# An adaLN transformer block on one core: Silu from PSUM, softmax without its maximum, one V transfer a tile, and a new order from a table of priorities

## The chip, the cores and the metric

The kernel runs on one core of a Trainium2 chip. The metric is the device time of one execution in microseconds. The kernel before took 284.76 us (median of 3 runs, 284.24 to 285.57).

Engines are named as in the profile: PE is the matrix engine, PEld its weight load, DVE the vector engine, ACT the scalar engine, POOL GpSimd, and SP the engine whose queue issues all DMA transfers here.

## The reference

Sequence 2048, model width 512, 32 heads of 16, FFN width 1792, all in bf16. A conditioning vector gives shift, scale and gate for each half of the block. Each token attends to 8 positions: itself and every second one before it.

```python
x = A_x
mod = (_silu(c) @ w_mod).reshape(c.shape[0], 6, 1, -1)
sa, ca, ga, sb, cb, gb = (mod[:, 0].copy(), ..., mod[:, 5].copy())
h = _layernorm(x, axis=-1) * (1 + ca) + sa
x = x + ga * _A_ref(h, A_wqkv, A_wo)
h = _layernorm(x, axis=-1) * (1 + cb) + sb
x = x + gb * _B_ref(h, B_w1, B_w3, B_w2)

# in _A_ref: W, dil = 8, 2
idx = pos[:, None] - off[None, :]            # off = arange(W) * dil
logits = jnp.einsum('bhsd,bhswd->bhsw', q, kg) * scale
attn = _softmax(jnp.where(mask, logits, -1e9), axis=-1)
o = jnp.einsum('bhsw,bhswd->bhsd', attn, vg)  # then @ wo
# in _B_ref
h = _silu(gate) * up                          # gate = x @ w1, up = x @ w3
out = jnp.einsum('bsf,fd->bsd', h, w2)
```

## The kernel before, in words

The work is cut into 16 tiles of 128 tokens and 4 chunks of 4 tiles. x stays in SBUF (`x_sb`).

**LN1 and projections, for each chunk.** DVE takes statistics (L520, L521), POOL the reciprocal root (L527, L529), DVE the norm (L536); PE transposes (L550) and ACT evicts with scale and shift (L558) into `h`. PE then computes q and k transposed (L585) and V by token (L604); ACT evicts them (L592, L593, L614). V goes to a scratch tensor in DRAM.

**Attention, for each tile.** DVE multiplies q with 8 shifted views of k in one instruction of 4096 columns (`sb_pq`, L633). PE sums over each head's 16 rows with an indicator matrix, 32 small matmuls (L642), into logits of 8 x 32 columns. DVE takes their maximum over a token (L652), ACT the exponential with that as bias (L655), DVE sum (L660), reciprocal (L663) and product (L665). The weights go to DRAM and come back laid out by (token, neighbour) on partitions (`sb_al`). V is read back in the same layout (`sb_vsh`): partition 8 s + w holds, for each of 8 groups g, the row of token 16 g + s minus 2 w. That takes 8 DMAs of 128 KB a tile. DVE multiplies weights into V (L680, again 4096 columns), PE sums over the neighbours with 32 small matmuls (L689), ACT evicts (L695), PE applies `wo` (L701, with the gate already multiplied in), and DVE adds to x (L705).

**FFN, for each chunk.** After LN2 of the 4 tiles come 14 units. In each, PE computes gate and up (L717, 4 matmuls of 512 columns each, into two PSUM banks); ACT evicts tanh(gate / 2) (L723) and up (L725); DVE forms (tanh + 1) * gate from PSUM (L727) and the product with up (L730). This is twice Silu(gate) * up; the half is in the gate `gb` (L514). W2 then takes 14 matmuls a tile (L741), and DVE adds x (L747) and SP stores.

**What sets the order.** Every operation is given an engine, a cost and a priority (`pr`). `Program.schedule` plays the program through with these costs: when an engine is free, it takes the operation of lowest `pr` whose inputs are ready and whose buffers (`Pool`) are free. The order that comes out is fixed for each engine; `synchronize` adds semaphore waits, and each engine runs its list strictly in order, SP too (all DMAs are issued at L123). Priorities before are formulas: attention of tile T at 1000 T, the FFN of a chunk 5500 behind its start, and so on. Buffers: 3 for `sb_vsh`, 3 for q, 6 for the normed x, 8 PSUM banks.

Of the kernel before, what the change touches and what calls it, by code (L numbers as in the profile page):

```python
# [11 lines left out]
P = 128  # L12
# [17 lines left out]
DMA_RATE = 260.0  # L30
# [31 lines left out]
class Op:  # L62
    __slots__ = ("eng", "fn", "cost", "pr", "deps", "vals", "n", "start", "end", "seen", "pos", "dma", "bytes",
                 "waits", "inc", "clock", "prev", "group")

    def __init__(self, eng, fn, cost, pr):
        self.eng, self.fn, self.cost, self.pr = eng, fn, cost, pr
        self.deps = {}
        self.vals = []
        self.prev = []  # L70
        self.end = None
        self.dma = False
        self.bytes = 0
        self.inc = None
        self.group = [self]


class Program:
# [7 lines left out]
    def op(self, eng, fn, cost, pr, r=(), w=(), part=(), after=(), dma=0):  # L86
        o = Op(eng, fn, cost, pr)
# [28 lines left out]
    def dma(self, out, in_, pr, nbytes, r=(), w=(), part=(), after=(), eng="sp", cost=450, group=None):  # L116
        nc = self.nc

        def fn(e):
            a = out() if callable(out) else out  # L120
            b = in_() if callable(in_) else in_
            with nc.allow_non_contiguous_dma(reason="layout"):
                return e.dma_start(a, b)  # L123

        o = self.op(eng, fn, cost, pr, r=r, w=w, part=part, after=after, dma=nbytes)
        if group is not None:
            group.append(o)
            o.group = group
        return o

    def schedule(self):
        ops = self.ops
        users = {o: [] for o in ops}
        missing = {}
        for o in ops:
            missing[o] = len(o.deps)
# [5 lines left out]
        ready_at = {o: 0 for o in ops}  # L142
        for o in ops:
            if not missing[o]:
                heapq.heappush(waiting[o.eng], (o.pr, o.n, o))
        busy = {e: 0 for e in ENGINES}
        self.order = {e: [] for e in ENGINES}
        self.placed = []
        dma_free = 0
        events = [0]  # L150
        done = []
        now = 0
        count = 0
        while count < len(ops):
            if not events:
                stuck = [(e, [(o.pr, o.n, [v.name for v in o.vals]) for _, _, o in sorted(waiting[e])[:3]]) for e in ENGINES]
                raise RuntimeError(f"stuck at {now}: {stuck}")
# [3 lines left out]
            while done and done[0][0] <= now:  # L161
                _, _, o = heapq.heappop(done)
                for v in o.vals:
# [3 lines left out]
                for u in users[o]:  # L167
                    missing[u] -= 1
                    ready_at[u] = max(ready_at[u], now)
                    if not missing[u]:  # L170
                        heapq.heappush(waiting[u.eng], (u.pr, u.n, u))
            for e in ENGINES:
                if busy[e] > now or not waiting[e]:
                    continue
                skipped, got = [], None
                while waiting[e]:
                    item = heapq.heappop(waiting[e])
                    o = item[2]
# [4 lines left out]
                    if all(len(p.free) >= k for p, k in need.items()):  # L183
                        got = o
                        break
                    skipped.append(item)
                for item in skipped:
                    heapq.heappush(waiting[e], item)
                if got is None:
                    continue  # L190
                o = got
                for v in o.vals:
# [3 lines left out]
                o.start = now  # L196
                busy[e] = now + o.cost
                if o.dma:
                    begin = max(now + o.cost, dma_free)
                    dma_free = begin + o.bytes / DMA_RATE  # L200
                    o.end = dma_free + LAT["sp"]
                else:
                    o.end = now + o.cost + LAT[e]
# [6 lines left out]
                count += 1  # L210
# [73 lines left out]
def bass_adaLN_cond__sliding_local_dilated__glu_gated_swiglu__prompt_kernel(  # L284
# [3 lines left out]
    with ctx:  # L288
        p = Program(nc, ctx)
        _build(p, *[_full_ap(t) for t in (A_x, A_wqkv, A_wo, B_w1, B_w3, B_w2, c, w_mod, out)])  # L290
        p.schedule()
# [4 lines left out]
MM = 216  # L296


def _build(p, A_x, A_wqkv, A_wo, B_w1, B_w3, B_w2, c, w_mod, out):
# [23 lines left out]
    atb = [sb([P, W, H], bf, f"attn{i}") for i in range(2)]  # L323
    alb = [sb([P, 8, H], bf, f"al{i}") for i in range(3)]
    exb = [sb([P, W, H], f32, f"ex{i}") for i in range(2)]
# [12 lines left out]
    smx = sb([P, 2], f32, "smx")  # L338
    ssum = sb([P, 2, H], f32, "ssum")
    rsum = sb([P, 2, H], f32, "rsum")  # L340
# [8 lines left out]
    NHH, NTMP = 20, 5  # L349
    region = sb([P, 1024 * NHH + 2048 * NTMP], dt.uint8, "region")  # L350
# [6 lines left out]
    thb = [at([P, 512], bf, f"th{i}", 1024 * NHH + 2048 * i) for i in range(NTMP)]  # L357
    ubb = [at([P, 512], bf, f"ub{i}", 1024 * NHH + 2048 * i + 1024) for i in range(NTMP)]
# [3 lines left out]
    wm_g = [at([P, KT, 512], bf, f"wm_g{i}", 12288 * i + 8192) for i in range(2)]  # L362

# [15 lines left out]
    smpool = Pool("sm", [(atb[i], exb[i], i) for i in range(2)])  # L379
    alpool = Pool("al", alb)  # L380
    otpool = Pool("ot", otb)
    hhpool = Pool("hh", hhb)
    tmppool = Pool("tmp", [(thb[i], ubb[i]) for i in range(NTMP)])

    TT = 1000.0

    def t_attn(T):
        return TT * T

    def t_ffn(cch, fi):  # L390
        return TT * (4 * cch + 5.5) + fi * (4 * TT / 20)

    def t_w2(T):
        return TT * (4 * (T // 4) + 5.5) + (14 + 1.5 * (T % 4)) * (4 * TT / 20)


    vc = Val("const")
    vident = Val("ident")
    p.op("pool", lambda e: e.memset(ones[:], 1.0), 150, -9e5, w=[vc])
    p.op("pool", lambda e: e.memset(ident[:], 0.0), 150, -9e5, w=[vident])  # L400
    p.op("pool", lambda e: e.affine_select(out=ident[:], in_=ident[:], compare_op=ALU.not_equal, fill=1.0, base=0,
                                           pattern=[[-1, P]], channel_multiplier=1), 300, -9e5, w=[vident])
# [26 lines left out]
    p.dma(bass.AP(cT, 0, [[KT, P], [1, KT]]), bass.AP(c.tensor, c.offset, [[1, P], [P, KT]]), -100, 1024, w=[vcT])  # L429
# [390 lines left out]
```

## Time and profile before

| what | value |
|---|---|
| time of 3 runs | 284.24, 284.76, 285.57 us |
| profiled execution, first to last instruction (span) | 281.8 us |
| median of the runs less that span | 3.0 us |
| mean granted PE clock of the profiled execution | 0.970 |
| PE, DVE, ACT, POOL busy | 249.3, 213.6, 134.7, 27.8 us |
| data moved by DMA | 36.29 MB |

The profile gives the span of the profiled execution and no separate device time for it; the three runs' median stands 3.0 us above it. Busy time is the union of an engine's instructions. PE's instructions overlap, so that an instruction's own length (386 ns for 512 columns) is more than the time from one to the next. The granted clock is the share of full speed at which PE was allowed to run. "Idle before" in a group is the time its engine stood still just ahead of its instructions, with what ended most of it. The chain of work that ended last is followed back from the last instruction, at each step to what released it.

### The profile page before, as it was taken

To read this page: it belongs to the slowest core of one execution; us is meant where nothing else is said; L and a number is where in the kernel's file an instruction comes from. 1 tells how busy PE (TensorE), PEld (TensorE's weight loads), DVE (VectorE), ACT (ScalarE), POOL (GpSimd) and SP (SyncE) were. 2 spreads that over 40 slices of the span, in tenths; PEclk is the share of its full clock that TensorE was granted. 3 is DMA by queue.
4 is the path that set the end of the run, shared out by engine and by line. 5 is a ranking of instruction groups with operands and counts; after the bars stand their busy time and mean duration, and the time that the engine had idled before them with its cause. 6 is when DMAs were issued, how large, how long until landed. Compare 5 with 4: busy or idle time off the path is not lost.

```text
span 281.8 us, 5292 instructions
## 1 busy us (share of the span) xinstructions
PE 249.3 (88%) x2152; PEld 127.8 (45%) x2152; DVE 213.6 (76%) x358; ACT 134.7 (48%) x228; POOL 27.8 (10%) x63
## 2 busy tenths in 40 slices
PE   0499995699799579999899999999999789999795
PEld 0345644247454324446445455554555344444342
DVE  4357989978998869989999998897787643466511
ACT  2347732753664255576144665850256502666400
POOL 4210010004410410100200101001020001000000
PEclk9999999589999959999999999999999999999999
DMA  5999994774656574622651655117200001000011
GB/s 167 364 288 385 338 350 129 192 216 135 165 167 170 180 192 103 182 62 40 191 147 66 158 151 152 19 31 188 50 0 12 9 19 37 21 0 0 0 37 40
DMA packets 55033, 36.29 MB, mean 129 GB/s; under 512 B 20432, under 2 KB 53984, under 8 KB 55008
## 3 DMA queue, kind: packets, MB, share of 16 engines
q1 hardware_dynamic: 55008, 35.95, 44.9%
q8 instruction: 17, 0.28, 0.4%
q14 instruction: 8, 0.07, 0.1%
HBM read 30.67 MB, written 5.26 MB: 128 GB/s over the span
## 4 chain that ended last, share of the span: by engine, by line
PE 73%; DVE 13%; ACT 4%; DMA 3%; SPq 3%; POOL 2%; issue 1%
PE pall L717 29%; PE pall L741 17%; PE pall L585 12%; DVE sb_vsh L680 5%; PE pall L604 4%; PE pall L701 3%; ACT sb_h L558 3%; PE pall L689 3%; SPq L123 3%; PE pall L642 2%; DMA sb_al<-a_scratch_dram 2%; PE pall L550 2%; POOL sb_rs L529 1%; DVE sb_th L727 1%; DVE sb_st L520 1%
## 5 line engine op out<-in xcount | busy, mean ns | idle before, releaser
L717 PE MATMUL pall<-sb_h,sb_w 128*128 128x512 bf16 x448 | 103.0, 386 | 2.8 <-ACT sb_h L558 2.8
L717 PEld LDWEIGHTS pall<-sb_h,sb_w 128*128 128x128 bf16 x448 | 43.5, 99 | 54.2 <-issue 3.3
L741 PE MATMUL pall<-sb_w,sb_hh 128*128 128x512 bf16 x224 | 49.7, 379 | 2.3 <-DVE sb_hh L730 2.3
L727 DVE SCALAR_TENSOR_TENSOR sb_th<-sb_th,pall 128x512 bf16<-128x512 bf16 x56 | 37.9, 682 | 17.7 <-ACT sb_ub L725 17.3
L723 ACT ACTIVATE sb_th<-pall 128x512 bf16<-128x512 f32 x56 | 33.5, 598 | 25.6 <-PE pall L717 25.6
L725 ACT ACTIVATE sb_ub<-pall 128x512 bf16<-128x512 f32 x56 | 33.5, 598 | 18.0 <-PE pall L717 18.0
L633 DVE TENSOR_TENSOR sb_pq<-sb_q,sb_kT 128x4096 bf16<-128x4096 bf16 x16 | 36.3, 2278 | 5.0 <-PE pall L642 3.3
L680 DVE TENSOR_TENSOR sb_vsh<-sb_vsh,sb_al 128x4096 bf16<-128x4096 bf16 x16 | 36.5, 2284 | 4.2 <-DMA sb_al<-a_scratch_dram 4.2
L558 ACT ACTIVATE sb_h<-pall,sb_modc 128x512 bf16<-128x512 bf16 x32 | 22.4, 777 | 35.5 <-PE pall L550 27.8
L585 PE MATMUL pall<-sb_h,sb_wqkv 128*128 128x512 bf16 x128 | 33.4, 422 | 5.4 <-ACT sb_h L558 4.7
L741 PEld LDWEIGHTS pall<-sb_w,sb_hh 128*128 128x128 bf16 x224 | 21.6, 98 | 28.1 <-DVE sb_hh L730 2.9
L527 POOL TENSOR_TENSOR sb_rs<-sb_mv,sb_cst 128x1 f32<-128x1 f32 (+1 forms) x23 | 9.5, 417 | 203.8 <-DVE sb_mv L521 203.8
L747 DVE TENSOR_TENSOR sb_o<-pall,sb_x 128x512 bf16<-128x512 f32 x16 | 11.0, 689 | 20.2 <-PE pall L741 20.1
L520 DVE BATCH_NORM_STATS2 sb_st<-sb_x 128x6 f32<-128x512 bf16 x32 | 21.2, 680 | 4.6 <-DMA sb_x<-in_A_x_dram 4.6
L585 PEld LDWEIGHTS pall<-sb_h,sb_wqkv 128*128 128x128 bf16 x128 | 12.8, 106 | 24.1 <-ACT sb_h L558 5.4
L730 DVE TENSOR_TENSOR sb_hh<-sb_th,sb_ub 128x512 bf16<-128x512 bf16 x56 | 23.0, 417 | 0.7
L695 ACT ACTIVATE sb_ot<-pall 128x512 bf16<-128x512 f32 x16 | 9.6, 597 | 27.2 <-PE pall L689 27.2
L550 PE MATMUL pall<-sb_ident,sb_xn 128*128 128x128 bf16 x128 | 11.7, 236 | 10.1 <-DVE sb_xn L536 8.2
L689 PE MATMUL pall<-sb_ind,sb_vsh 128*128 128x16 bf16 x512 | 15.2, 169 | 3.7 <-DVE sb_vsh L680 1.9
L689 PEld LDWEIGHTS pall<-sb_ind,sb_vsh 128*128 128x128 bf16 x512 | 14.5, 96 | 8.5 <-DVE sb_vsh L680 3.0
L642 PE MATMUL pall<-sb_E,sb_pq 128*128 128x32 bf16 x512 | 14.8, 176 | 3.7 <-DVE sb_pq L633 3.7
L701 PE MATMUL pall<-sb_wo,sb_ot 128*128 128x512 bf16 x64 | 16.5, 379 | 1.6 <-ACT sb_ot L695 1.6
(56 smaller groups left out, 178.1 us busy)
## 6 DMA issues: line engine op xcount, KB each, us to landing
sb_vsh<-v_scratch_dram SPq DMA_DIRECT2D x128, 128.0 KB, 2.7
sb_wm_s<-in_w_mod_dram SPq DMA_DIRECT2D x2, 1024.0 KB, 8.7
sb_w<-in_B_w_dram SPq DMA_DIRECT2D x4, 512.0 KB, 9.1
v_scratch_dram<-sb_v SPq DMA_DIRECT2D x16, 128.0 KB, 2.3
out_dram<-sb_o SPq DMA_DIRECT2D x16, 128.0 KB, 1.7
sb_w<-in_B_w_dram SPq DMA_DIRECT2D x1, 1792.0 KB, 11.9
sb_wqkv<-in_A_wqkv_dram SPq DMA_DIRECT2D x3, 512.0 KB, 8.4
sb_x<-in_A_x_dram SPq DMA_DIRECT2D x3, 512.0 KB, 9.1
```

The lines of the kernel that those rows point to most:

```text
L520: p.op("dve", lambda e: e.bn_stats(st[:, i, :], x_sb[:, T, :]), 670, pr, r=[vx[T]], w=[vs])
L558: return e.activation(vh.at[:, ft, :], b[:, j * 512:(j + 1) * 512], ACT.Identity, bias=modc[:, 8 * which + ft:8 * which + ft + 1], scale=m ...
L585: ins = e.matmul(bank(vp), wqkv[:, t, col:col + P], vh.at[:, t, :], start=(t == 0), stop=(t == KT - 1))
L633: return e.tensor_tensor(vp.at[:], in0, in1, ALU.mult)
L680: return e.tensor_tensor(v_w, v_w, a_w, ALU.mult)
L689: ins = e.matmul(b[:, ft * P + 16 * g:ft * P + 16 * g + 16], vv.at[:, g, ft * P:(ft + 1) * P], ind[:], start=True, stop=True)
L701: ins = e.matmul(bank(vy), vt.at[:, ft, :], wo[:, ft, :], start=(ft == 0), stop=(ft == KT - 1))
L717: ins = e.matmul(bank(vp), wt[:, t, fi * P:(fi + 1) * P], vh.at[:, t, :], start=(t == 0), stop=(t == KT - 1))
L723: p.op("act", lambda e: e.activation(vt.at[0][:], bank(vgp), ACT.Tanh, scale=0.5), 540, pr, r=[vgp], w=[vt])
L725: p.op("act", lambda e: e.activation(vt.at[1][:], bank(vup), ACT.Copy), 540, pr, r=[vup], w=[vu], part=[vt])
L727: p.op("dve", lambda e: e.scalar_tensor_tensor(vt.at[0][:], vt.at[0][:], 1.0, bank(vgp), op0=ALU.add, op1=ALU.mult), 700, pr, r=[vgp, vt], ...
L741: ins = e.matmul(bank(vz), vhh[(cch, fi)].at[:, tt * P:(tt + 1) * P], w2[:, fi, :], start=(fi == 0), stop=(fi == NF - 1))
```

## The change

**SwiGLU.** ACT computes Silu(gate) from PSUM (L762 of the kernel after) and DVE multiplies it with up straight from PSUM (L765). The eviction of up, one DVE pass and the half in `gb` go. Silu and Exp are in different tables of ACT, so the build puts in table loads where the order changes from one to the other.

**Softmax.** The maximum and the bias go. Tiles are taken alone (0, 1, 2, 3) or in pairs; a pair shares a PSUM bank, one Exp and one set of DVE operations. The sum over 8 neighbours is three adds of halves.

**V.** Groups are now 8 tokens apart inside, so that partition 8 s + w reads 8 rows that follow each other: one DMA of 128 runs of 8 KB. The weights' store and the eviction of the sum (L733) permute to match. `sb_vsh` has 2 buffers, and a third one in the place of the q/k weights, free once all projections are done.

**Order.** FFN groups are of 2, 4, 4, 4 and 2 tiles. q has 4 buffers. LN2's and LN1's reciprocal roots are all taken by tile. W2's 14 matmuls a tile are two operations of 7. Priorities come from a table of numbers, one for each operation; the player now also knows the table load, looks 250 ns ahead and keeps some operations in one piece. The loads of late weights wait for the q k product of a tile (`LATE`).

```diff
-DMA_RATE = 260.0
+DMA_RATE = 320
+TABLE_LOAD = 1300
+LOOK = 250
...
+FFN = [[0, 1], [2, 3, 4, 5], [6, 7, 8, 9], [10, 11, 12, 13], [14, 15]]
+BLOCKS = [[[0]], [[1]], [[2], [3]], [[4, 5], [6, 7]], [[8, 9], [10, 11]], [[12, 13], [14, 15]]]
+LATE = {"wms1": 0, "wmg1": 1, "w13_0": 0, "w13_1": 1, "w13_2": 2, "w13_3": 3, "w2": 4}
...
-    qb = [sb([P, KT, 512], bf, f"q{i}") for i in range(3)]
+    qb = [sb([P, KT, 512], bf, f"q{i}") for i in range(4)]
...
-    xnb = [sb([P, D], bf, f"xn{i}") for i in range(6)]
-    vb = [sb([P, D], bf, f"v{i}") for i in range(4)]
-    vshb = [sb([P, 8, D], bf, f"vsh{i}") for i in range(3)]
+    xnb = [sb([P, D], bf, f"xn{i}") for i in range(5)]
+    vb = [sb([P, D], bf, f"v{i}") for i in range(3)]
+    vshb = [sb([P, 8, D], bf, f"vsh{i}") for i in range(2)]
...
+    vsh_x = nc.alloc_sbuf_tensor_at("sb_vshx", [P, 8, D], bf, offset=nc.lookup_mloc(wqkv).addr)
...
+        for Ts, vl, ve in zip(groups, vls, ves):
+            n = len(Ts) * W * H
+            ins = e.activation(ve.at[1].rearrange("p t w h -> p (t w h)")[:, 0:n], bank(vl)[:, 0:n], ACT.Exp)
...
+        o = p.op("dve", lambda e: e.tensor_tensor(ve.at[2][:, 0:n], ve.at[1][:, 0:n, 0:4], ve.at[1][:, 0:n, 4:8], ALU.add),
+                 75 + 134 * n, k, r=[ve], w=[vs1], lead=o)
...
-        for g in range(8):
-            p.dma(lambda g=g: vv.at[:, g, :], bass.AP(v_dram, (PAD + T * P + 16 * g) * D, [[D, 16], [-DIL * D, W], [1, D]]),
-                  pr - 1, 131072, r=[vv_dram[T]] + ([vv_dram[T - 1]] if T else [vvpad]), part=[vv], cost=450, group=grp)
+        p.dma(lambda: vv.at[:].rearrange("p g d -> p (g d)"),
+              bass.AP(v_dram, (PAD + T * P) * D, [[8 * D, 16], [-DIL * D, W], [1, 8 * D]]), ("vl", T), 1048576,
+              r=[vv_dram[T]] + ([vv_dram[T - 1]] if T else [vvpad]), w=[vv])
...
-        p.op("act", lambda e: e.activation(vt.at[0][:], bank(vgp), ACT.Tanh, scale=0.5), 540, pr, r=[vgp], w=[vt])
-        p.op("pe", lambda e: mm(e, vup, w3), 4 * MM, pr, r=[vh, vw13[g]], w=[vup])
-        p.op("act", lambda e: e.activation(vt.at[1][:], bank(vup), ACT.Copy), 540, pr, r=[vup], w=[vu], part=[vt])
...
+        p.op("act", lambda e: e.activation(vt.at[:, 0:n], bank(vgp)[:, 0:n], ACT.Silu), c_act(n), k, r=[vgp], w=[vt],
+             table="silu")
+        p.op("pe", lambda e: mm(e, vup, w3), 4 * c_mm(n), k, r=[vh, vw13[g]], w=[vup])
+        p.op("dve", lambda e: e.tensor_tensor(vh_.at[:, 0:n], vt.at[:, 0:n], bank(vup)[:, 0:n], ALU.mult), c_dve(n), k,
+             r=[vt, vup], w=[vh_])
...
+        "ac": [330157, 178789, 212700, 341252, 350924, 288664, 457781, 340148, 470407, 470586, 420151, 440561, 89399, 476673, 167761, 440406],
```

**Where it moves instructions.** On PE, before, the last rows ahead of the first FFN matmul (`sb_w` with `sb_h`, L717) are V (L604), logits (L642), sums over V (L689), wo (L701) and transposes (L550):

```order
L604 MATMUL pall<-sb_wqkv,sb_h 128x512 x16
L689 MATMUL pall<-sb_ind,sb_vsh 128x16 x32
L642 MATMUL pall<-sb_E,sb_pq 128x32 x32
L701 MATMUL pall<-sb_wo,sb_ot 128x512 x4
L689 MATMUL pall<-sb_ind,sb_vsh 128x16 x32
L550 MATMUL pall<-sb_ident,sb_xn 128x128 x4
L701 MATMUL pall<-sb_wo,sb_ot 128x512 x4
L642 MATMUL pall<-sb_E,sb_pq 128x32 x32
L550 MATMUL pall<-sb_ident,sb_xn 128x128 x4
L717 MATMUL pall<-sb_h,sb_w 128x512 x20
```

After, the same place on PE, with L600 for q/k, L620 for V, L727 for sums over V, L740 for wo and L756 for the FFN:

```order
L740 MATMUL pall<-sb_wo,sb_ot 128x512 x4
L620 MATMUL pall<-sb_wqkv,sb_h 128x512 x4
L600 MATMUL pall<-sb_h,sb_wqkv 128x512 x8
L574 MATMUL pall<-sb_ident,sb_xn 128x128 x4
L600 MATMUL pall<-sb_h,sb_wqkv 128x512 x8
L574 MATMUL pall<-sb_ident,sb_xn 128x128 x4
L600 MATMUL pall<-sb_h,sb_wqkv 128x512 x8
L620 MATMUL pall<-sb_wqkv,sb_h 128x512 x4
L727 MATMUL pall<-sb_ind,sb_vsh 128x16 x32
L756 MATMUL pall<-sb_h,sb_w 128x256 x56
L660 MATMUL pall<-sb_E,sb_pq 128x32 x32
L740 MATMUL pall<-sb_wo,sb_ot 128x512 x4
```

Before, five tiles have been through wo when the FFN begins; after, two have, the FFN begins with a group of those two, and all q and k stand ahead of it.

On ACT, before, inside the first FFN chunk (`sb_th` the tanh, `sb_ub` the up half, `sb_ot` the evicted sum over V):

```order
L723 ACTIVATE sb_th_72<-pall 128x512
L725 ACTIVATE sb_ub_77<-pall 128x512
L655 ACTIVATE sb_ex<-pall,sb_smx 128x256
L723 ACTIVATE sb_th_73<-pall 128x512
L725 ACTIVATE sb_ub_78<-pall 128x512
```

After, inside the second FFN group, ACT has (`sb_sg` the Silu, `sb_ex` the Exp of two pairs of tiles):

```order
L762 ACTIVATE sb_sg_70<-pall 128x512
L674 ACT_TABLE_LOAD
L674 ACTIVATE sb_ex<-pall 128x512 x2
L733 ACTIVATE sb_ot<-pall 128x512
L762 ACT_TABLE_LOAD
L762 ACTIVATE sb_sg_71<-pall 128x512
L762 ACTIVATE sb_sg_72<-pall 128x512
```

The up half is gone from ACT, four tiles share one place for the Exp, and two table loads stand around it.

In SP's queue, before, around the first V transfers (`sb_vsh`), the weights' stores (to `a_scratch`) and loads (`sb_al`):

```order
L123 DMA sb_vsh<-v_scratch_dram 128x1x512 x8
L123 DMA sb_al<-a_scratch_dram 128x8x32
L123 DMA v_scratch_dram<-sb_v 128x512 x4
L123 DMA sb_vsh<-v_scratch_dram 128x1x512 x8
L123 DMA a_scratch_dram<-sb_attn 128x256
L123 DMA sb_vsh<-v_scratch_dram 128x1x512 x8
```

After, in SP's queue (DMAs at L133), the third and later V transfers:

```order
L133 DMA sb_al<-a_scratch_dram 128x8x32
L133 DMA v_scratch_dram<-sb_v 128x512
L133 DMA sb_vsh<-v_scratch_dram 128x1x4096 x2
L133 DMA a_scratch_dram<-sb_attn 16x8x256 x2
L133 DMA sb_al<-a_scratch_dram 128x8x32
L133 DMA v_scratch_dram<-sb_v 128x512 x3
```

Eight issues a tile became one, so a load of weights has far fewer issues ahead of it.

More of the change, by code (lines that the diff above doesn't have):

```diff
@@ L114, in op, with dma @@
         return o
-    def dma(self, out, in_, pr, nbytes, r=(), w=(), part=(), after=(), eng="sp", cost=450, group=None):
+    def dma(self, out, in_, key, nbytes, r=(), w=(), part=(), after=(), eng="sp", cost=450, group=None):
         nc = self.nc
@@ L209, in schedule @@
                 self.placed.append(o)
-                count += 1
+                for u in users[o]:
+                    missing[u] -= 1
+                    ready[u] = max(ready[u], busy[e] if e == u.eng == "pe" else o.end)
+                    if not missing[u]:
+                        waiting[u.eng].append(u)
+                        heapq.heappush(events, max(now, ready[u] - LOOK))
         self.span = max(o.end for o in ops)
@@ L543, in ln_T @@
             vt = Val("ps_tr", psum)
-            for tt in range(4):
+            for tt in range(n):
                 def tr(e, tt=tt, vt=vt, half=half):
```

516 lines of the change are left out of this document (265 added, 251 removed), and 27 rows, old and new, of the table vhh.

## The prediction

> **What bounds the kernel now.** I read the page's first lines, then a table by stage, then the chain of work that ended last, then the groups by form. The page:
>
> ```profile
> span 281.8 us, 5292 instructions
> PE 249.3 (88%) x2152; PEld 127.8 (45%) x2152; DVE 213.6 (76%) x358; ACT 134.7 (48%) x228; POOL 27.8 (10%) x63
> PEclk9999999589999959999999999999999999999999
> ```
>
> PE is the busiest engine, but a busy PE can be a slow one: the granted clock was about half in one slice near 50 us and in one near 103 us. The table by stage (columns: stretch, its length, PE, PEld, DVE, ACT, POOL, clock, DMA share, GB/s):
>
> ```profile
> 14.30:43.30 29.00, 28.90 (x280) 15.48 (x280) 22.82 (x43) 16.45 (x28) 2.43 (x4) 1.00 1.07 334
> 43.30:58.10 14.80, 9.44 (x71) 4.28 (x68) 14.80 (x19) 7.38 (x13) 0.00 (x0) 0.66 0.64 169
> 58.10:100.60 42.50, 34.81 (x518) 20.71 (x516) 36.86 (x51) 21.83 (x38) 11.37 (x12) 0.98 0.61 170
> 100.60:137.20 36.60, 35.57 (x301) 17.71 (x302) 32.75 (x54) 20.13 (x36) 1.85 (x6) 0.93 0.47 117
> 137.20:227.20 90.00, 87.70 (x713) 44.91 (x710) 77.07 (x130) 44.96 (x77) 6.53 (x15) 1.00 0.32 85
> ```
>
> From 43.3 to 58.1 DVE has no idle time and PE waits for it. From 58.1 to 100.6, where the FFN matmuls begin, PE is idle for 7.7 us and DVE for 5.6. What both wait for there is in the chain (start, length, what; whole run, pieces left out):
>
> ```profile
> 4.38 1.19 DVE sb_st L520 x2
> ...
> 14.31 8.48 PE pall L585 x32
> ...
> 41.87 0.81 PE pall L642 x32
> ...
> 85.50 0.60 SPq L123
> ...
> 86.78 2.52 DMA sb_al<-a_scratch_dram
> 89.32 2.29 DVE sb_vsh L680
> ...
> 161.59 0.78 PE pall L689 x32
> ...
> 175.27 0.67 PE pall L550 x12
> ...
> 240.57 24.19 PE pall L717 x112
> ...
> 278.91 0.69 DVE sb_o L747
> ```
>
> The weights' transfer (sb_al) stands behind V re-layout issues in SP's queue; these are 128 at 598 ns, 77 us of SP:
>
> ```profile
> L123 SPq DMA_DIRECT2D sb_vsh<-v_scratch_dram x128: 514/598/1631, 43.9 to 193.9; - x128
> ```
>
> **The floor.** The chain's dense PE pieces give matmul prices: 24.19/112 = 216 ns at 512 columns, 0.67/12 = 56 at 128, 0.81/32 = 25.3 for logits, 0.78/32 = 24.4 for the sums over V. By the code there are 936 of the first (448 + 224 FFN, 192 q/k/v, 64 wo, 8 gates), 128, 512 and 512, and 64 tiny ones that I put at 25 ns: 202.2 + 7.2 + 13.0 + 12.5 + 1.6 = 236.5 us. Ahead of the first projection at 14.31 PE works 1.7 us of this (16 transposes, 32 tiny ones), so the head costs 12.6; the tail from 278.91 costs 2.9. That is 252.0 of 281.8: 29.8 us are lost in the middle, to waits and slow clock. The change can win these and hardly more.
>
> **The change part by part.** Rows for the prices (line, shapes, count | busy, mean ns | idle before):
>
> ```profile
> L727 DVE SCALAR_TENSOR_TENSOR sb_th<-sb_th,pall 128x512 bf16<-128x512 bf16 x56 | 37.9, 682 | 17.7 <-ACT sb_ub L725 17.3
> L680 DVE TENSOR_TENSOR sb_vsh<-sb_vsh,sb_al 128x4096 bf16<-128x4096 bf16 x16 | 36.5, 2284 | 4.2 <-DMA sb_al<-a_scratch_dram 4.2
> L633 DVE TENSOR_TENSOR sb_pq<-sb_q,sb_kT 128x4096 bf16<-128x4096 bf16 x16 | 36.3, 2278 | 5.0 <-PE pall L642 3.3 <-ACT sb_kT L593 1.8
> L725 ACT ACTIVATE sb_ub<-pall 128x512 bf16<-128x512 f32 x56 | 33.5, 598 | 18.0 <-PE pall L717 18.0
> L730 DVE TENSOR_TENSOR sb_hh<-sb_th,sb_ub 128x512 bf16<-128x512 bf16 x56 | 23.0, 417 | 0.7
> L558 ACT ACTIVATE sb_h<-pall,sb_modc 128x512 bf16<-128x512 bf16 x32 | 22.4, 777 | 35.5 <-PE pall L550 27.8 <-DVE sb_modc L498 7.7
> L520 DVE BATCH_NORM_STATS2 sb_st<-sb_x 128x6 f32<-128x512 bf16 x32 | 21.2, 680 | 4.6 <-DMA sb_x<-in_A_x_dram 4.6
> L529 POOL TENSOR_TENSOR sb_rs<-sb_rs,sb_cst 128x1 f32<-128x1 f32 x20 | 13.2, 664 | 1.3
> L536 DVE TENSOR_SCALAR sb_xn<-sb_x,sb_mv,sb_rs 128x512 bf16<-128x512 bf16 x32 | 12.3, 404 | 3.9 <-POOL sb_rs L529 3.8
> L747 DVE TENSOR_TENSOR sb_o<-pall,sb_x 128x512 bf16<-128x512 f32 x16 | 11.0, 689 | 20.2 <-PE pall L741 20.1
> L660 DVE TENSOR_REDUCE sb_ssum<-sb_ex 128x32 f32<-128x256 f32 x16 | 9.2, 583 | 0.7 <-ACT sb_ex L655 0.7
> L655 ACT ACTIVATE sb_ex<-pall,sb_smx 128x256 f32<-128x256 f32 x16 | 7.5, 478 | 4.2 <-DVE sb_smx L652 4.2
> L652 DVE TENSOR_REDUCE sb_smx<-pall 128x1 f32<-128x256 f32 x16 | 6.6, 416 | 1.5 <-PE pall L642 1.0 <-DMA a_scratch_dram<-sb_attn 0.4
> L665 DVE TENSOR_TENSOR sb_attn<-sb_ex,sb_rsum 128x256 bf16<-128x256 f32 x16 | 6.6, 415 | 0.1
> L663 DVE RECIPROCAL sb_rsum<-sb_ssum 128x32 f32<-128x32 f32 x16 | 5.3, 339 | 0.0
> L521 DVE BATCH_NORM_AGGREGATE sb_mv<-sb_st 128x2 f32<-128x6 f32 x32 | 4.9, 166 | 0.1
> L784 DVE TENSOR_TENSOR sb_w<-sb_w,sb_gb_bc 128x3584 bf16<-128x3584 bf16 x2 | 4.0, 2008 | 0.0
> L466 ACT ACT_TABLE_LOAD x1 | 1.3, 1283 | 0.8 <-PEq L805 0.8
> ```
>
> *SwiGLU.* DVE gives up L727 and L730 (60.9 us) for one product from PSUM a unit: 42 of 512 columns at 689 (L747's form) and 28 of 256, which no row shows; between half of 689 and all of it, I take 415 (L665, 256 columns): 28.9 + 11.6 = 40.5, so 20.4 saved. ACT gives up one of two evictions (67 us) for 42 × 598 + 28 × 478 = 38.5, if Silu is priced like the tanh and copy that it replaces; saved 28.5. The scaling of the gate by 0.5 goes, 0.3.
>
> *Softmax.* DVE gives up 6.6 + 9.2 + 5.3 + 6.6 = 27.7. It gets ten groups (four of one tile, six of two) of three adds, a reciprocal and a product. The adds lie between 166 (a tiny operation) and 415; in between by size, a single costs 290 + 227 + 195 + 339 + 415 = 1.47 us, a pair about 415 + 290 + 227 + 500 + 689 = 2.12: 18.6 in all, 9.1 saved. DVE comes to about 213.6 − 20.4 − 9.1 − 0.3 = 184 us, well under the 237 of PE.
>
> *Silu beside Exp.* ACT's order now has five more table loads, one ahead of the first Silu and two pairs inside the second FFN group. At 1283 ns they are 6.4 us of an engine that falls to 134.7 − 28.5 + 6.4, about 113. On the path: in a pair ACT is away for 2 × 1.28 + 2 × 0.60 = 3.8 us, while PE fills one unit (two of eight PSUM banks) in 8 × 0.216 = 1.73 and runs on for two units, 3.5 us. I charge 1 us a pair, 2 in all; bounds 0 and 3.8 a pair. The Trainium skill ("ScalarE: Activation LUTs", What ACT_TABLE_LOAD costs and the rule on batching by set) counts 2.66 us a switch, with a drain that this trace's single load does not show; by it the sum would be 5.4 us more. That is a rival below.
>
> *One V transfer a tile.* 112 issues of 598 ns leave SP, 67 us, so the weights no longer queue there. The transfer itself is now 1 MB in one piece, in runs of 8 KB that no row shows. Its neighbours (size, median us to landing):
>
> ```profile
> sb_vsh<-v_scratch_dram SPq DMA_DIRECT2D x128, 128.0 KB, 2.7
> sb_wm_s<-in_w_mod_dram SPq DMA_DIRECT2D x2, 1024.0 KB, 8.7
> sb_w<-in_B_w_dram SPq DMA_DIRECT2D x1, 1792.0 KB, 11.9
> ```
>
> Bounds 2.7 and 11.9; I take 8.7, the row of the same size. The Trainium skill ("DMA: Bandwidth & Descriptors", Bandwidth) measured 6.15 us for 1 MB, which would only leave more slack. A buffer then cycles in 0.6 + 8.7 + 2.3 + 0.8 = 12.4 us; with two (a third only once all projections are done), 16 tiles take 99 us. They have from about 50 to 207 us, so this costs nothing at 8.7; the cover ends at 157/8 − 3.7 = 16 us.
>
> *Order and groups.* Until the first FFN matmul PE now has all q/k, 56 of 64 V matmuls, 8 logits, 3 sums and 2 wo: 128 + 56 + 8 + 8 = 200 × 0.216 + 56 transposes × 0.056 + 256 × 0.0253 + 96 × 0.0244 + 32 × 0.025 = 56 us after 14.31, so 70 at the earliest and 72 with the slow start kept (8.48 − 32 × 0.216 = 1.6). In before it came at 100.6. DVE owes by then, up to the norm of tile 1: 18 × (0.680 + 0.166) + 18 × 0.404 + 8 × 2.278 + 4 × 1.47 + 2.12 + 2 × 2.284 + 2 × 2.008 + 2 × 0.689, the wo scaling 1.2 (by size from L784) and some fifteen tiny ones at 0.166 (2.5): 62.5 us from 4.4 (its first statistics), with the 4.6 wait for x about 71.5. PE and DVE arrive together, so each is late now and then: I charge 3 us, between 0 and the 13.1 that PE idles there now (5.4 + 7.7). The second group needs tile 5 through residual 0.69, statistics 0.85, POOL about 1.0, norm 0.40, and four evictions 3.1: 6.0 us, against 21 W2, 3 logits and 1 V step of PE, 7.8 us. I charge 2 for it and its like, between 0 and 6, and 1 for the rest. Matmuls of 256 columns: between 56 and 216, by size 109; 224 × 0.109 against 112 × 0.216 is +0.2.
>
> **Sum.** 236.5 + 0.2 + 12.6 + 2.9 = 252.2; waits 1.6 + 3 + 2 + 2 + 1 = 9.6; span 261.8. The runs' median of before is 284.76, 3.0 above the profiled span, so **264.8 us**.
>
> **The rivals.** *The waits stay in the early stage* (20%): the order is fixed ahead, in each queue one late step holds all behind it, and the clock halves again as at 50 us. Two thirds of the 29.8 remain, 19.9: 252.2 + 19.9 + 3.0 = 275. For it: DVE and PE arrive together, and W2's transfer must land before its scaling; against it: SP's 67 us are gone. *Nearly all waits go* (7%): only 1.6 is left, 256.8. *Table switches stall ACT for 2.66 us* (7%): 5.4 more, 270.2; the trace's one load has no neighbour to judge by. *The V transfer is slow* (4%), the one on the other side: above 16 us each further us costs 8 (16 tiles, two buffers). To pass 286.2 it needs (286.2 − 264.8)/8 = 2.7 more, so slower than 18.7 us or 56 GB/s. For it: no row has 8 KB runs. Against it: 170 GB/s in the same stage now.
>
> **Numbers.** The forecast itself, 259 to 271, has 62%. The range 258.5 to 275 leaves out half of the first two rivals and the last, under 20%. A measurement of this kernel tells about 0.5%, 1.4 us, from no change: faster 0.94, same 0.02, slower 0.04.
>
> **What would show it.** Right: first 512- or 256-column FFN matmul near 75 us, no half-clock slice after 20 us, DVE near 184 us, SP free of V issues, V transfers of 7 to 10 us, ACT loads without PE gaps over 1 us. Wrong: PE idle before 75 us by over 6 us, or DVE waiting on sb_vsh or sb_w transfers, or PE waiting for Silu after a load.

## The result, and the profile after

The changed kernel takes 262.78 us (median of 4 runs, 261.81 to 263.44), the kernel before 284.77 (4 runs of the same session, 284.24 to 285.57): a ratio of 0.922, 95% interval 0.919 to 0.925. The forecast was 264.8 us in a range from 258.5 to 275. The profiled execution is that of 261.81 us, with a span of 259.8.

The page of the changed kernel:

```profile
span 259.8 us, 5381 instructions
PE 242.0 (93%) x2264; PEld 138.2 (53%) x2264; DVE 191.5 (74%) x301; ACT 109.1 (42%) x189; POOL 36.8 (14%) x81
PEclk9999999799999999999999999999999999999999
PE 83%; DMA 9%; DVE 4%; ACT 1%; POOL 1%; SPq 1%; issue 0%
```

The low clock slice near 103 us is gone and that near 50 us is shallower; the chain that ended last is 83% PE. Its pieces that stand out, with the first FFN piece, a long one and the last (start, length, what):

```profile
3.13 5.99 DMA sb_wm_s<-in_w_mod_dram
...
13.81 6.07 PE pall L600 x20
...
29.60 17.85 DMA sb_wm_s<-in_w_mod_dram
...
71.20 2.23 POOL sb_rs L555
...
77.69 6.13 PE pall L756 x56
...
198.82 20.72 PE pall L756 x96
...
248.16 2.62 PE pall L756 x24
```

The first FFN matmul starts at 77.6 us (its piece in the chain at 77.69) in place of 100.7. Ahead of it one transfer holds the chain for 17.85 us, the weights of the second modulation. The table by stage (stretch, its length, PE, PEld, DVE, ACT, POOL, clock, DMA share, GB/s):

```profile
14.30:77.70 63.40, 59.18 (x642) 33.12 (x641) 54.75 (x85) 40.51 (x71) 17.74 (x25) 0.97 0.92 249
77.70:175.00 97.30, 97.30 (x1012) 57.83 (x1011) 88.18 (x120) 41.50 (x69) 6.04 (x16) 1.00 0.63 136
175.00:227.00 52.00, 52.00 (x377) 26.31 (x376) 29.60 (x47) 17.51 (x31) 6.41 (x12) 1.00 0.19 48
```

From 77.7 on PE has no idle time, while DVE is busy for 88.2 of 97.3 us. After its first FFN matmul the kernel before needed 281.8 − 100.7 = 181.1 us, this one 259.8 − 77.6 = 182.2. That is not the same work. The kernel before, ahead of its first FFN matmul and from there to the tail:

```profile
14.30:100.70 86.40, 73.18 (x861) 40.49 (x862) 74.58 (x111) 45.75 (x79) 13.80 (x16) 0.93 0.77 225
100.70:278.90 178.20, 173.03 (x1244) 84.95 (x1244) 132.11 (x222) 84.71 (x144) 9.12 (x22) 0.99 0.27 72
```

At the prices of the prediction these stretches held 65.5 and 169.2 us of PE work, so 20.9 and 9.0 us were lost in them. In the changed kernel the same two stretches hold 56.0 and 179.0 us of work, since less of the attention has run when the FFN begins, and take 63.9 and 179.2. So the early stage lost 7.9 us in place of 20.9, and what follows 0.2 in place of 9.0: some 13 us of the gain lie ahead of the first FFN matmul and some 9 behind it.

### The profile page after: what moved, and what is told of

The parts are those of the page before. It is cut to its first block, busy times and chain, and to the rows that moved or that the text cites. A ratio compares the mean times of both kernels' runs of the same rounds, so it can differ in the third digit from the quotient of the medians.

```text
span 259.8 us, 5381 instructions
## 1 busy us (share of the span) xinstructions
PE 242.0 (93%) x2264; PEld 138.2 (53%) x2264; DVE 191.5 (74%) x301; ACT 109.1 (42%) x189; POOL 36.8 (14%) x81
## 4 chain that ended last, share of the span: by engine, by line
PE 83%; DMA 9%; DVE 4%; ACT 1%; POOL 1%; SPq 1%; issue 0%
PE pall L756 37%; PE pall L777 19%; DMA sb_wm_s<-in_w_mod_dram 9%; PE pall L600 8%; PE pall L740 5%; PE pall L727 5%; PE pall L660 3%; PE pall L620 3%; PE pall L574 2%; DVE sb_pq L651 2%; ACT sb_h L582 1%; POOL sb_rs L555 1%; SPq L133 1%; PE pall L520 1%; DVE sb_st L550 0%
## 5 line engine op out<-in xcount | busy, mean ns | idle before, releaser
L756 PE MATMUL pall<-sb_h,sb_w 128*128 128x512 bf16 (+1 forms) x560 | 101.0, 336 | 0.0
L756 PEld LDWEIGHTS pall<-sb_h,sb_w 128*128 128x128 bf16 x560 | 53.9, 98 | 41.3
L762 ACT ACTIVATE sb_sg<-pall 128x512 bf16<-128x512 f32 (+1 forms) x70 | 35.4, 512 | 69.1 <-PE pall L756 69.0
L765 DVE TENSOR_TENSOR sb_hh<-sb_sg,pall 128x512 bf16<-128x512 bf16 (+1 forms) x70 | 38.6, 577 | 25.4 <-PE pall L756 21.8
L553 POOL TENSOR_TENSOR sb_rs<-sb_mv,sb_cst 128x1 f32<-128x1 f32 x32 | 14.3, 446 | 160.3 <-DVE sb_mv L551 160.1
L600 PE MATMUL pall<-sb_h,sb_wqkv 128*128 128x512 bf16 x128 | 33.1, 404 | 3.1 <-ACT sb_h L582 3.1
L718 DVE TENSOR_TENSOR sb_vsh<-sb_vsh,sb_al 128x4096 bf16<-128x4096 bf16 x13 | 29.6, 2285 | 3.2 <-DMA sb_al<-a_scratch_dram 2.2
L582 ACT ACTIVATE sb_h<-pall,sb_modc 128x512 bf16<-128x512 bf16 (+1 forms) x36 | 23.8, 730 | 18.9 <-PE pall L574 13.8
L550 DVE BATCH_NORM_STATS2 sb_st<-sb_x 128x6 f32<-128x512 bf16 x32 | 21.7, 679 | 3.2 <-DMA sb_x<-in_A_x_dram 2.9
L600 PEld LDWEIGHTS pall<-sb_h,sb_wqkv 128*128 128x128 bf16 x128 | 12.5, 103 | 17.1 <-ACT sb_h L582 3.4
L555 POOL TENSOR_TENSOR sb_rs<-sb_rs,sb_cst 128x1 f32<-128x1 f32 x32 | 20.4, 637 | 2.5
L733 ACT ACTIVATE sb_ot<-pall 128x512 bf16<-128x512 f32 x16 | 9.6, 598 | 21.8 <-PE pall L727 19.8
L660 PEld LDWEIGHTS pall<-sb_E,sb_pq 128*128 128x128 bf16 x512 | 15.0, 96 | 3.2 <-ACT sb_h L582 0.3
L740 PE MATMUL pall<-sb_wo,sb_ot 128*128 128x512 bf16 x64 | 15.9, 379 | 0.0
L620 PE MATMUL pall<-sb_wqkv,sb_h 128*128 128x512 bf16 x64 | 15.8, 379 | 0.0
L574 PEld LDWEIGHTS pall<-sb_ident,sb_xn 128*128 128x128 bf16 x128 | 9.2, 103 | 12.0 <-DVE sb_xn L558 7.9
```

Source lines behind the costliest of these rows:

```text
L574: ins = e.transpose(b[:, col:col + P], vns[tt].at[:, ft * P:(ft + 1) * P], ident[:])
L582: return e.activation(vh.at[:, ft, 0:n * P], b[:, j * 512:j * 512 + n * P], ACT.Identity, bias=modc[:, 8 * which + ft:8 * which + ft + 1], ...
L600: ins = e.matmul(bank(vp), wqkv[:, t, col:col + P], vh.at[:, t, :], start=(t == 0), stop=(t == KT - 1))
L620: ins = e.matmul(bank(vp), vh.at[:, t, tt * P:(tt + 1) * P], wqkv[:, t, 2 * D:3 * D], start=(t == 0), stop=(t == KT - 1))
L660: ins = e.matmul(b[:, c0:c0 + H], vp.at[:, w, ft, :], E_sb[:, ft, :], start=(ft == 0), stop=(ft == KT - 1))
L718: return e.tensor_tensor(v_w, v_w, a_w, ALU.mult)
```

## The experiments

**Theories.** *Saved work:* the parts that take work from DVE, ACT and SP made the gain. *Order:* the new order alone made it. *Early stage and cover* (the prediction's): PE waited ahead of the first FFN for DVE and for SP's issues; relief there and the order remove that, and what is left is waits in that stage.

All runs in one table; the ratio is to the kernel before on the same chip, the last column is the start of the first FFN matmul in the trace.

| kernel | median us | ratio (95%) | first FFN |
|---|---|---|---|
| before | 284.77 | 1 | 100.7 |
| before, one V transfer | 288.87 | 1.015 (1.008 to 1.023) | 100.7 |
| before, Silu from PSUM | 282.10 | 0.994 (0.990 to 0.997) | 100.7 |
| before, all three parts | 284.52 | 0.997 (0.993 to 1.001) | 100.3 |
| the same, projections early | 285.04 | 1.001 (0.997 to 1.005) | 98.5 |
| the same, groups 2,4,4,4,2 | 279.86 | 0.982 (0.974 to 0.990) | 88.6 |
| the same, both | 284.31 | 0.998 (0.994 to 1.002) | 91.5 |
| changed | 262.78 | 0.922 (0.919 to 0.925) | 77.6 |
| changed, V in 8 pieces | 261.46 | 0.918 (0.911 to 0.925) | 76.1 |
| changed, product twice | 282.13 | 0.991 (0.987 to 0.994) | 77.5 |
| changed, Silu twice | 264.61 | 0.931 (0.925 to 0.937) | 78.8 |
| changed, max pass back | 264.97 | 0.933 (0.928 to 0.938) | 79.5 |
| changed, one table | 262.19 | 0.924 (0.919 to 0.929) | 78.2 |
| changed, second modulation's weights early | 258.15 | 0.911 (0.905 to 0.916) | 73.7 |

The rows were measured on several chips: a difference to the changed kernel is given by the medians, and by the ratios times 284.8 where that differs. The variants of the changed kernel keep its instructions in its order, written out as a list, so that nothing but the edit moves. Those of the kernel before let its own rules make the order.

### The saved parts in the order of before

The edits: V's 8 transfers become one, with the weights' store permuted to match; Tanh, a copy and two DVE passes become Silu and one product; the maximum, the bias and the reduce become three adds, for one tile at a time.

```diff
-        for g in range(8):
-            p.dma(lambda g=g: vv.at[:, g, :], bass.AP(v_dram, (PAD + T * P + 16 * g) * D, [[D, 16], [-DIL * D, W], [1, D]]),
-                  pr - 1, 131072, ..., part=[vv], cost=450, group=grp)
+        p.dma(lambda: vv.at[:].rearrange("p g d -> p (g d)"),
+              bass.AP(v_dram, (PAD + T * P) * D, [[8 * D, 16], [-DIL * D, W], [1, 8 * D]]), pr - 1, 1048576, ..., w=[vv])
```

```diff
-        p.op("act", lambda e: e.activation(vt.at[0][:], bank(vgp), ACT.Tanh, scale=0.5), 540, pr, r=[vgp], w=[vt])
+        p.op("act", lambda e: e.activation(vt.at[0][:], bank(vgp), ACT.Silu), 540, pr, r=[vgp], w=[vt])
...
-        p.op("dve", lambda e: e.tensor_tensor(vh_.at[:], vt.at[0][:], vt.at[1][:], ALU.mult), 430, pr, r=[vs, vu, vt], w=[vh_])
+        p.op("dve", lambda e: e.tensor_tensor(vh_.at[:], vt.at[0][:], bank(vup), ALU.mult), 700, pr, r=[vup, vt], w=[vh_])
```

One V transfer alone:

> The kernel before with the single V transfer alone; its own rules make the order. Theory 1: the SP wait ahead of the first FFN matmul goes (PE idle 7.7 us from 58 to 100.6, and the half clock after it), the DVE-bound stretch from 43 to 58 stays: 274 to 281. Theory 2 (order): 282 to 286. Theory 3 (saved work): 270 to 276.

Silu alone:

> The kernel before with Silu from PSUM alone (one eviction and one DVE pass fewer per unit, table loads added). Theory 1: these units start at 100 us, behind the stage that loses time, and PE was busy from there on in 35.6 of 36.6 and 87.7 of 90 us, so 1 to 4 us at most: 281 to 285. Theory 2: 283 to 286. Theory 3: DVE's 20 us and ACT's 28 us of relief show as 8 us or more: below 277.

All three:

> The kernel before with all three saved parts (single V transfer, Silu from PSUM, softmax without max pass, one tile at a time), its own rules making the order, groups of four tiles as before. Theory 1: about half of the gain, since the DVE-bound early stage stays with q/k and V work spread as before: 268 to 277. Theory 2 (order): 280 to 285. Theory 3 (saved work): 261 to 266, as good as the changed kernel.

Measured: 1.5% slower, 0.6% faster, no change. No theory had the slowdown; mine had forecast 274 to 281 us for the single transfer. The theory of saved work falls, and mine with it where it gave half of the gain to the three parts. With all three, DVE's busy time falls from 213.6 to 189.3 us, and the first FFN matmul stands where it was. The end of that stage in the chain, with all three parts:

```profile
73.76 7.28 DMA sb_vsh<-v_scratch_dram
81.06 2.29 DVE sb_vsh L676
...
86.19 9.46 DMA a_scratch_dram<-sb_attn
95.68 0.39 ACT sb_ex L646
...
96.12 1.03 PE pall L640 x32
...
100.25 1.89 PE pall L714 x4
```

SP's queue there (start, length of the issue):

```profile
84.40 0.51 SPq L123 DMA_DIRECT2D sb_vsh<-v_scratch_dram  x1
86.19 0.56 SPq L123 DMA_DIRECT2D a_scratch_dram<-sb_attn  x1
86.80 1.03 SPq L123 DMA_DIRECT2D v_scratch_dram<-sb_v  x1
```

SP is free now, but the 64 KB of attention weights, issued 1.8 us behind 1 MB of V, land after 9.46 us; their median rose from 2.1 us to 5.6. The next Exp waits for the buffer that they leave, and ACT holds the transposes' evictions behind it. The wait on issues had become a wait on transfers.

### Two rules of the order, by hand

Both stand on the kernel with all three parts. The early projections also need a fourth q buffer and give up one of six `xn` buffers; with the small groups the FFN weights are due earlier.

```diff
-        base = t_attn(4 * cch) - 4 * TT
+        base = t_attn(cch) - TT + 100 if cch else -4 * TT
```

```diff
+    FG = [[0, 1], [2, 3, 4, 5], [6, 7, 8, 9], [10, 11, 12, 13], [14, 15]]
+    FS = {0: 3.5, 2: 7.5, 6: 11.5, 10: 15.5, 14: 19.5}
...
-        return TT * (4 * cch + 5.5) + fi * (4 * TT / 20)
+        return TT * FS[Ts[0]] + fi * (len(Ts) * TT / 20)
```

> The kernel before with the three saved parts (which by themselves gave 284.5 us), and now all projections early under its own rules: q, k and V of chunk c are due with tile c-1 in place of tile 4(c-1); groups of four tiles as before. Theory Q (the early q/k matmuls are the part of the order that counts: PE has 41 us of projections that wait for no attention and fill the stage where it was late): most of the 20 us lost ahead of the first FFN matmul go, 266 to 273. Theory G (the small first group counts: FFN work is there earlier): 281 to 286. Theory S (neither rule; only an order searched instruction by instruction does it): 279 to 286.

> The kernel before with the three saved parts and FFN groups of 2, 4, 4, 4, 2 tiles under its own rules; projections due as before. Theory Q: PE is short of work between 45 and 100 us as before, 279 to 286. Theory G: the first FFN matmul comes 20 us earlier with 28 matmul pairs of work behind it, 268 to 276. Theory S: 279 to 286.

> Both at once under its own rules: projections early and groups of 2, 4, 4, 4, 2, with the three saved parts. Theory Q: as with the early projections alone, give or take 3 us: 264 to 273. Theory G: as with the groups alone, 266 to 276. If they only work together: 262 to 268 here and over 277 for each alone. Theory S: above 275.

Measured: nothing, 1.8%, nothing. The small groups keep a quarter of the gain (first FFN at 88.6), less than the 268 to 276 of theory G; Q falls, and the two don't add up: of these theories S is nearest. The rules as I wrote them are one choice of due times; that no simple rule could do it is not shown. Nor does a run take apart what came with the new order: the list itself, the pairs of tiles in the softmax, the buffers.

### V in eight pieces, in the new order

```diff
-        p.dma(lambda: vv.at[:].rearrange("p g d -> p (g d)"),
-              bass.AP(v_dram, (PAD + T * P) * D, [[8 * D, 16], [-DIL * D, W], [1, 8 * D]]), ("vl", T), 1048576, ...
+                return [e.dma_start(vv.at[:, g, :], bass.AP(v_dram, (PAD + T * P + g) * D, [[8 * D, 16], [-DIL * D, W], [1, D]]))
+                        for g in range(8)]
```

> The changed kernel with its order kept instruction by instruction, but V read back in 8 transfers of 128 KB a tile (1 KB runs) in place of one of 1 MB: 112 SP issues of about 0.6 us return, 67 us. Theory 1 (SP's issues held up the early stage, and the single transfer removed that wait): the weights and the later loads queue behind 4.8 us a tile again; two to four tiles lie ahead of or at the first FFN matmul, so 2 to 8 us come back: 265 to 271. Theory 2 (the new order alone did it, the saved work hardly matters): within 1.5 us of 262.8. Theory 3 (the saved work did it, the order hardly matters): most of the 9 to 11 us of SP wait return, 270 or more.

Measured 261.46, an interval that takes in the changed kernel's: 112 more issues cost nothing here, as the theory of order alone had it. What the single transfer does to its neighbours, first in the changed kernel and then with 8 pieces (KB each, median us to landing):

```profile
sb_vsh<-v_scratch_dram SPq DMA_DIRECT2D x13, 1024.0 KB, 8.1
sb_wm_s<-in_w_mod_dram SPq DMA_DIRECT2D x2, 1024.0 KB, 11.9
v_scratch_dram<-sb_v SPq DMA_DIRECT2D x16, 128.0 KB, 6.3
a_scratch_dram<-sb_attn SPq DMA_DIRECT2D x16, 64.0 KB, 3.2
```

```profile
sb_vsh<-v_scratch_dram SPq DMA_DIRECT2D x104, 128.0 KB, 2.7
sb_wm_s<-in_w_mod_dram SPq DMA_DIRECT2D x2, 1024.0 KB, 5.7
v_scratch_dram<-sb_v SPq DMA_DIRECT2D x16, 128.0 KB, 3.2
a_scratch_dram<-sb_attn SPq DMA_DIRECT2D x16, 64.0 KB, 2.2
```

With the same instructions in the same order, V's stores take twice as long from issue to landing beside 1 MB pieces. The medians of the weight loads are of two each: the first, ahead of any V, takes 6.0 and 5.7 us, the second 17.8 and 5.7. But part of this wait has only changed its place: with 8 pieces SP is busy with 16 V issues for 11.0 us first, issues that second load at 40.2 in place of 29.6 us, and it lands only 1.5 us earlier. The Trainium skill ("DMA: Bandwidth & Descriptors", Bandwidth) advises batching transfers to 1 MiB or more; these two runs show no gain in time from it, and longer landings of the small transfers in the same queue.

### Does the order need the saved work?

The product repeated (DVE), and as its counterpart Silu repeated (ACT); each writes the same tile a second time.

```diff
+        o = p.op("dve", lambda e: e.tensor_tensor(vh_.at[:, 0:n], vt.at[:, 0:n], bank(vup)[:, 0:n], ALU.mult), ...
         p.op("dve", lambda e: e.tensor_tensor(vh_.at[:, 0:n], vt.at[:, 0:n], bank(vup)[:, 0:n], ALU.mult), ...
```

```diff
+        o = p.op("act", lambda e: e.activation(vt.at[:, 0:n], bank(vgp)[:, 0:n], ACT.Silu), ...
         p.op("act", lambda e: e.activation(vt.at[:, 0:n], bank(vgp)[:, 0:n], ACT.Silu), ...
```

> The changed kernel, order kept, with the SwiGLU product computed twice (the same DVE instruction repeated, 70 more: 42 at 0.683 and 28 at 0.417, 40 us of DVE, as much as one of before's two passes and a bit more). If the saved DVE work is what makes the new order possible: DVE was busy in 88 of the 97 us from 77.7 to 175, 21 us more fall in there, so PE waits 8 to 18 us: 271 to 281. If the order does it alone and DVE has slack: 262 to 266.

> The changed kernel, order kept, with Silu computed twice (the same ACT instruction repeated, 70 more: 42 at 0.597 and 28 at 0.384, 35.8 us of ACT, as much as one of before's two evictions). It holds the gate's PSUM bank longer by one instruction, as the doubled product did for the other bank. If DVE's load alone made the doubled product cost 19.4 us: ACT is busy in 109 of 260 us and takes it, 262 to 266. If a longer stay in PSUM, or a chain longer by one instruction in a fixed order, is what cost it there: as much here, 272 to 282.

Measured 282.13 and 264.61. The same stages, first with the product twice, then with Silu twice:

```profile
77.70:175.00 97.30, 87.42 (x911) 51.27 (x924) 94.28 (x140) 36.90 (x61) 6.06 (x16) 0.98 0.57 128
175.00:227.00 52.00, 49.13 (x368) 24.21 (x372) 44.46 (x66) 15.33 (x25) 6.42 (x12) 0.97 0.27 61
```

```profile
77.70:175.00 97.30, 95.37 (x991) 56.96 (x1004) 89.23 (x119) 59.00 (x106) 6.04 (x16) 1.00 0.62 136
175.00:227.00 52.00, 51.61 (x392) 26.25 (x397) 29.90 (x48) 28.22 (x48) 6.41 (x12) 1.00 0.20 49
```

With the product twice the first FFN matmul comes at the same time (77.5) and everything is lost behind it: DVE fills up, PE idles for 97.3 − 87.4 = 9.9 us in the first stretch. PE's waits for DVE over the whole run (us, times, longest); in the first stretch they are 5.3, 1.5 and 2.0 us, in the order of these lines:

```profile
PE pall L667 <- DVE sb_vsh L658: 5.3, 5, 1.7
PE pall L721 <- DVE sb_hh L709: 5.3, 5, 2.1
PE pall L600 <- DVE sb_pq L591: 2.2, 3, 1.0
```

Silu twice adds 34.6 us to ACT and costs 1.8 us by the medians, 2.5 by the ratios. In its trace 1.2 us stand ahead of the first FFN matmul (78.8), where no Silu runs and the second modulation's weights land that much later. So it is DVE's load and not a longer stay in PSUM or a longer chain. The new order needs room on DVE: with 38.9 us more work there it loses 19.4 of the 22.0 us of gain. The change had saved DVE only 22.1 us, and the new order at just that load wasn't run. In proportion 22.1 us would cost 11 us, an estimate; by it the order alone keeps about half of the gain, where the saved work alone gave none. So the order does not stand without any saved work, but alone it may be worth half of the gain.

### The other parts

The max pass back, one for each softmax group:

```diff
+            o = p.op("dve", lambda e, ...: e.tensor_reduce(smx[:, T:T + 1], bank(vl)[:, 0:n], AX.X, ALU.max, negate=True), ...
-                ins = e.activation(ve.at[1].rearrange("p t w h -> p (t w h)")[:, 0:n], bank(vl)[:, 0:n], ACT.Exp)
+                ins = e.activation(ve.at[1].rearrange("p t w h -> p (t w h)")[:, 0:n], bank(vl)[:, 0:n], ACT.Exp,
+                                   bias=smx[:, Ts[0]:Ts[0] + 1])
```

> The changed kernel, order kept, with the max pass back: ten DVE reductions (four at 0.42, six pairs near 0.7, 5.9 us in all), one for each softmax group, and the Exp with that as bias, 93 ns more each. If DVE is near the bound (38.9 us more of DVE work cost 19.4 us in the run with the product twice, 0.5 us per us): 264.5 to 267. If DVE's slack takes it: 262.3 to 264.

```profile
L615 DVE TENSOR_REDUCE sb_smx<-pall 128x1 f32<-128x512 f32 x6 | 3.9, 686 | 0.3 <-PE pall L601 0.3
L615 DVE TENSOR_REDUCE sb_smx<-pall 128x1 f32<-128x256 f32 x4 | 1.6, 418 | 0.0
```

Measured 264.97: 2.2 us (3.0 by the ratios) for 5.5 us of DVE, near the 0.5 us per us of the doubled product. In its trace 1.9 us stand ahead of the first FFN matmul (79.5); of these up to 1.2 can be the spread that Silu twice showed there. And without table switches; Tanh stands in Silu's place, so this kernel computes another function:

```diff
-        p.op("act", lambda e: e.activation(vt.at[:, 0:n], bank(vgp)[:, 0:n], ACT.Silu), ...
+        p.op("act", lambda e: e.activation(vt.at[:, 0:n], bank(vgp)[:, 0:n], ACT.Tanh), ...
```

> The changed kernel, order kept, with Tanh in Silu's place (another function is computed), so that no table is switched between Exp and the gate. If the five loads of 1.28 us lie hidden, as the trace of the changed kernel shows PE without a gap there: 262 to 263.6, no change. If each switch held the path by 2.66 us as forecast in one rival: 5 us or more less, below 258.

Measured 262.19, no change: the five loads lie hidden.

### The early stage's last wait

```diff
-LATE = {"wms1": 0, "wmg1": 1, "w13_0": 0, "w13_1": 1, "w13_2": 2, "w13_3": 3, "w2": 4}
+LATE = {"w13_0": 0, "w13_1": 1, "w13_2": 2, "w13_3": 3, "w2": 4}
```

The two loads then stand in SP's list ahead of the first V store.

> The changed kernel, order kept but for two SP issues: the second modulation's weights (1 MB and 0.5 MB) are issued ahead of the first V store in place of behind the first logits' product. Theory W (what is left of the early loss is that transfer, on which PE waits 3.9 us at 43.7, and the half clock for some 7 us after it): both go, 4 to 5 us: 257.5 to 259.5. Rival (the earlier 1.5 MB push back the first V stores and the FFN weights, so the wait moves there, or DVE, busy 29.0 of the 34.7 us from 43 to 77.7, is the next to bind): 261 to 265.

The chain's PE pieces around the wait, first in the changed kernel, then here (start, busy us):

```profile
42.94 0.95 PE L660 MATMUL pall<-sb_E,sb_pq 128*128 128x32 bf16 x32 [0.24 <-DVE sb_pq L651]
47.59 0.98 PE L520 MATMUL pall<-sb_csT_bf,sb_wm_s 128*128 128x1 bf16 x32 [3.70 <-DMA sb_wm_s<-in_w_mod_dram]
48.43 1.87 PE L600 MATMUL pall<-sb_h,sb_wqkv 128*128 128x512 bf16 x4
```

```profile
43.92 0.95 PE L600 MATMUL pall<-sb_E,sb_pq 128*128 128x32 bf16 x32 [0.23 <-DVE sb_pq L591]
44.72 0.94 PE L460 MATMUL pall<-sb_csT_bf,sb_wm_s 128*128 128x1 bf16 x32
45.74 0.81 PE L540 MATMUL pall<-sb_h,sb_wqkv 128*128 128x512 bf16 x3
```

Measured 258.15 us: 4.6 less than the changed kernel by the medians, 3.3 by the ratios, 3.9 by the profiled spans (255.9), and the intervals (0.905 to 0.916 against 0.919 to 0.925) don't meet. The wait and the half clock behind it, 3.4 us and not the 7 expected, are gone (granted clock 1.000 in the profiled execution), the first FFN matmul comes at 73.7. This is the fastest version found.

## Why the prediction was right, point by point

**Floor.** PE work from 77.69 to 256.86 was 179.2 us against 179.0 at the prices of the sum, so 216 and 109 ns held (96 matmuls of 512 columns in 20.72 us, 56 of 256 in 6.13). Head: 13.81 − 1.7 = 12.1, 0.5 less than charged. Tail 2.9.

**Early stage.** Charged 1.6 + 3, forecast start of the FFN 72 to 75. PE has 56.0 us of work from 13.81 to the start at 77.69, which means 6.2 us beyond the slow start's 1.75, in place of 3. The step that failed is "PE and DVE arrive together, so each is late now and then": DVE is busy for only 54.8 of the 63.4 us of this stage, and PE waited for a transfer that the sum didn't look at.

```profile
PE pall L520 <- DMA sb_wm_s<-in_w_mod_dram: 4.9, 2, 3.7
```

The change issues those weights at 29.6 in place of 14.5 us, behind a tile's q·k product, and the prediction put nothing down for that. PE idles for 3.7 us and then runs at a granted clock of 0.51 from 47.8 to 51.2, some 1.7 us more by that share, an estimate. The last experiment puts 3.3 to 4.6 us on the whole. The other such moment is small: PE is idle for 0.28 us up to 73.92, where POOL is late by the 2.23 us of its piece in the chain above.

**Late waits.** Charged 2 for table loads, 2 for the second group, 1 for the rest; measured 0.2 in all. The loads took 1283 ns each and cost the path nothing:

```profile
L762 ACT ACT_TABLE_LOAD x3 | 3.8, 1283 | 0.1
L674 ACT ACT_TABLE_LOAD x2 | 2.6, 1283 | 0.0
```

Of the rivals, the one that kept two thirds of the waits in the early stage asked for 19.9 us of them and got 8.1 in the whole; the slow V transfer needed 18.7 us; the 2.66 us a switch is out. The Trainium skill ("ScalarE: Activation LUTs", What ACT_TABLE_LOAD costs) counts a drain beside the load; no idle time of ACT ahead of these loads shows one, and the run without switches is no faster.

**The total** fits since the errors offset: waits 8.1 in place of 9.6, the head 0.5 less, so 259.8 against 261.8 of span. That the sum came out is no proof of its parts: the early stage lost more than was charged, the late waits less. Two of the prediction's own signs of being right failed with it: a stretch at half clock near 50 us was left, and DVE was busy for 191.5 us in place of about 184.

**Prices.** Silu 597 and 384 ns (598 and 478 taken), the 256-column product 417 (415), the V transfer 8.1 (8.7), slowest 15.9. The Trainium skill's 6.15 us for 1 MB ("DMA: Bandwidth & Descriptors", Bandwidth) lies below the fastest of these 16, 6.7 us, which ran beside other transfers. The Trainium skill's figure there is the busy time of a transfer issued from GpSimd; these are times from SP's issue to landing. DVE came to 191.5 us, not 184. The lengths of its instructions did fall as counted, from 233.6 to 203.7 us in the trace (29.9; 29.8 forecast); but neighbours overlap by about 80 ns, 20.0 us in all before and 12.2 after, and busy time is the union. Fewer, less densely packed instructions overlap less.

**What the prediction didn't ask.** It took the 67 us of SP issues for one of the bounds and counted their going against its first rival. In this stage they could be put back without cost in the new order, and taken away without gain in the old one. SP stood in the chain of before for 30% of 80 to 101 us, but what took its place there was as long.

## What to carry to other kernels

A row at the end of the chain tells what is late, not what is gained by removing it: three real savings, 24 us of DVE and 67 of SP among them, moved nothing in the old order. The new order lets PE start its long work earlier and run it without gaps, and for that it needs the room on DVE, but not the 67 us of SP. Undo each part in the final order and also try each in the old one: here DVE's saving was worth next to nothing in the old and about half of the gain, by the estimate above, in the final one. When an operation's place in a queue changes, price its transfer too: here the last wait of the stage was a load moved behind another.

## What the runs showed of the hardware

- A 64 KB store issued behind 1 MB reads took a median of 5.6 us to land, where it had taken 2.1 beside 128 KB reads; in one fixed order, with V in 1 MB pieces against 8 of 128 KB, V's stores took 6.3 against 3.2 us from issue to landing. A 1 MB weight load took 17.8 us issued right behind two 1 MB pieces at 29.6, and 5.7 issued behind 16 pieces of 128 KB at 40.2.
- After PE had idled 3.7 us from 43.9, its matmuls of 512 columns stood 0.43 us apart until 51, twice the 0.216, at a granted clock of 0.51; with that wait gone they stood 0.216 apart there, at 1.00.
- POOL's 128x1 operations took 0.26 (L553) and 0.55 us (L555) without DVE's scaling beside them, and 1.9 and 2.2 us beside it (W2, 128x3584, at 66.22 and 70.99 in the trace, 2.0 us each):

```profile
66.38 1.88 POOL L553 TENSOR_TENSOR sb_rs<-sb_mv,sb_cst 128x1 f32<-128x1 f32 x1 [19.92 <-DVE sb_mv L551]
68.34 0.55 POOL L555 TENSOR_TENSOR sb_rs<-sb_rs,sb_cst 128x1 f32<-128x1 f32 x1
70.86 0.26 POOL L553 TENSOR_TENSOR sb_rs<-sb_mv,sb_cst 128x1 f32<-128x1 f32 x1 [1.97 <-DVE sb_mv L551]
71.20 2.22 POOL L555 TENSOR_TENSOR sb_rs<-sb_rs,sb_cst 128x1 f32<-128x1 f32 x1
```
